# Small jobs off VectorE, double buffers for finished rows, two more closing steps and earlier gathers in a fused top-32 attention and top-1 expert kernel

## The chip, the cores and the metric

One core of one Trainium2 chip. Times are device microseconds (us) of one launch. TensorE (PE) does matmuls and transposes, VectorE (DVE), ScalarE (ACT) and GpSimd (POOL) do the rest, and SyncE (SP) issues most transfers. Indirect transfers (gathers and scatters by a list of rows) are issued by GpSimd.

## The reference

```python
scores = scale * np.matmul(q, k.transpose(0, 1, 3, 2))          # q, k, v: [8, 8, 576, 64], float32
kth = np.partition(scores, -32, axis=-1)[..., -32:-31]
scores = np.where(scores >= kth, scores, -1e9)
attn = softmax(scores)
x = np.matmul(attn, v).transpose(0, 2, 1, 3).reshape(4608, 512)
logits = x @ w_gate                                             # 8 experts
gate_w = softmax(logits) at the largest logit
out[token] = gate_w * (np.maximum(x @ w1[e], 0) @ w2[e])        # e: that expert; w1 [512, 1024], w2 [1024, 512]
```

So each row of scores keeps its 32 largest, and each token then goes through one of eight experts. All is float32; the kernel gets that precision from matmuls on split values (a high and a low part).

## The kernel before, in words

**Attention.** 144 steps, nine for each of 16 groups of head pairs; 18 steps make one batch. A step is spread over the loop by stages, so that iteration t works on several steps at once: TensorE computes the scores of step t+3 (L354, the rest in L367 and L373), ScalarE copies them to SBUF (L356, L375), VectorE finds the 32nd largest value of each row by MAX8 and match-replace rounds (L988 with 21 MAX8 a step, L994), GpSimd makes thresholds of it (L990), ScalarE takes the sign of score minus threshold (L429) and GpSimd adds it to the scores (L430), TensorE transposes (L443, L446), ScalarE takes the exponential (L451) and TensorE multiplies with the values (L460, L475).

**Small jobs.** Between these, small jobs run as generators in lanes: `prep` (inputs), `sums` (row sums of the exponentials), `rows` (finished rows of x are transposed, scaled and stored, with their gate logits), `find`, `redo` and `patch` (a batch's few rows whose mask by the approximate threshold was wrong are found, done again and scattered over the stored rows), `route` (each token's expert and slot in a table). Every `yield need(...)` names what the next piece costs on an engine, and `advance()` hands a piece out when the step has room (LIMITS L44, due times DUE L43). The pieces go through queues (`pe`, `vec`, `act`, `pool`) that are flushed into the engines at fixed places; all of them are recorded as L252. Instructions of an engine run in the order in which they were issued.

**Close and experts.** The loop runs on for closing iterations after the last scores; in those with t < steps + TADV one `advance(None)` hands out a piece of each lane without limits (L1009). Then the experts run by units: five early ones (units 0 to 4) with tokens of the first batches, so that they can start before the last batches are routed, then whole experts and leftovers. Unit 0 has its inputs (tiles kt) gathered and its weights split in the attention's close; other units gather theirs to gx (L841) by tables that `route` has scattered (L812). A unit has eight chunks: `hidden` (L1107), `project` (L1122), weight splits (L919, L921, L922), and in the later chunks the transposes of the next unit's inputs (L1087 to L1089). The remaining small jobs of the last batches run between these chunks. `fetch(u + 1)` is called from a unit's second chunk on, and `fetch(u + 2)` in its seventh chunk, though only for units that are not early (L1175).

The names that matter below: r_fl (in `find`, a list of slots), r_v and found (in `redo`, a count of values found again), hist and cum (in `route`, tokens per expert), vq and its sum with nr (in `sums`), xm, xl, lp and lpl (in `rows`), r_xa and r_hm (in `patch`).

## Time and profile before

| | us |
|---|---|
| three runs | 1322.58, 1326.03, 1327.28 (median 1326.03) |
| the profiled execution, its own time | 1327.61 |
| its span in the trace | 1325.8 |
| busy: TensorE / VectorE / ScalarE / GpSimd | 1265.1 / 1037.6 / 823.2 / 905.2 |
| mean granted TensorE clock | 0.985 |

Busy times are of the whole span, with attention up to about 785 us, a close and the experts' start up to about 820 us, and the experts from there. An engine that waits inside an instruction for something that the profile doesn't show counts as busy.

### The profile page before, as it was taken

What the parts mean: (1) busy time and instruction counts of PE and PEld (TensorE: products, weight loads), DVE (VectorE), ACT (ScalarE), POOL (GpSimd) and SP (SyncE); (2) the same over time, 40 slices, a digit from 0 to 9 for tenths busy, and PEclk for the clock granted to TensorE, in tenths of its full rate; (3) what the DMA queues carried; (4) which work ended last, traced back from release to release, by engine and by line L of the source; (5) the groups of instructions that cost most, each with busy time, mean ns of one, the idle gap of its engine ahead of it and who ended that gap; (6) DMA issues with size and microseconds to landing.
All of it is one profiled execution on the core that took longest, in us unless ns stands there. A gap on an engine that the chain in (4) does not pass through costs nothing.

```text
span 1325.8 us, 32793 instructions
## 1 busy us (share of the span) xinstructions
PE 1265.1 (95%) x9688; PEld 1007.6 (76%) x9688; DVE 1037.6 (78%) x6838; ACT 823.2 (62%) x1691; POOL 905.2 (68%) x1272
## 2 busy tenths in 40 slices
PE   5999999999999999999999988998999999999997
PEld 3677777777677777777676767888799898989996
DVE  6999999999999999999998985745673333345664
ACT  3998898888788788788887863433233323233442
POOL 3777886887887887888877886754654333245654
PEclk8999999999999999999999997999999999999999
DMA  6656564664655655555654434735654333246774
GB/s 169 202 161 175 172 206 142 174 187 147 174 173 162 169 166 161 170 167 162 173 164 134 150 119 113 221 91 159 157 178 154 109 109 115 88 151 189 219 218 124
DMA packets 271244, 211.25 MB, mean 159 GB/s; under 512 B 136216, under 2 KB 214216, under 8 KB 271056
## 3 DMA queue, kind: packets, MB, share of 16 engines
q1 hardware_dynamic: 260320, 185.92, 48.3%
q0 software_dynamic: 9504, 22.86, 5.4%
q8 instruction: 78, 1.28, 0.4%
q14 instruction: 110, 0.90, 0.2%
q10 hardware_dynamic: 1232, 0.30, 0.1%
HBM read 102.49 MB, written 107.90 MB: 159 GB/s over the span
## 4 chain that ended last, share of the span: by engine, by line
PE 62%; DVE 19%; issue 6%; POOL 5%; ACT 5%; DMA 2%; SPq 1%; POOLq 0%; ACTq 0%; DVEq 0%
PE ph L1107 16%; PE y L1122 15%; DVE cand L988 9%; PE ps L354 6%; PE px L460 6%; PE pt L252 5%; PE tt L446 5%; DVE cand L994 3%; DVE vq L994 3%; PE tt L443 3%; PE px L475 2%; ACT sg L429 2%; POOL sb L430 2%; PE mt L1087 1%; PE px L367 1%
## 5 line engine op out<-in xcount | busy, mean ns | idle before, releaser
L430 POOL TENSOR_TENSOR sb<-sb,sg 128x576 f32<-128x576 f32 x288 | 369.8, 1292 | 133.8 <-ACT sg L429 131.1
L988 DVE MAX8 cand<-sb 128x8 f32<-128x52 f32 (+2 forms) x3024 | 368.9, 211 | 2.8 <-ACT sb L356 2.2
L922 POOL TENSOR_TENSOR wl<-r,wh 128x512 fp32r<-128x512 f32 x110 | 142.4, 1296 | 221.2 <-DVE wh L921 211.8
L429 ACT ACTIVATE sg<-sb,nb 128x576 int8<-128x576 f32 x288 | 223.1, 775 | 23.6 <-POOL nb L990 21.5
L460 PEld LDWEIGHTS px<-et,rv 128*64 128x64 f32 x2688 | 132.1, 138 | 122.6 <-issue 57.5
L1108 ACT ACTIVATE hh<-ph 128x320 fp32r<-128x320 f32 (+3 forms) x136 | 58.3, 428 | 240.8 <-PE ph L1107 218.1
L994 DVE MAX8 vq<-cand 128x8 f32<-128x22 f32 (+7 forms) x1152 | 205.2, 207 | 0.8 <-DVE cand L994 0.8
L451 ACT ACTIVATE et<-tt 128x1152 f32<-128x1152 f32 x144 | 163.1, 1132 | 44.3 <-PE tt L446 43.5
L354 PE MATMUL ps<-qk 64*128 64x512 f32 (+1 forms) x576 | 183.9, 646 | 3.1 <-ACT sb L356 2.5
L1109 DVE SCALAR_TENSOR_TENSOR hl<-ph,hh 128x320 fp32r<-128x320 f32 (+3 forms) x136 | 65.1, 479 | 149.9 <-ACT hh L1108 128.9
L460 PE MATMUL px<-et,rv 128*64 128x128 f32 (+1 forms) x2688 | 166.7, 268 | 14.8 <-ACT xt L252 4.7
L356 ACT ACTIVATE sb<-ps 128x1024 f32<-128x1024 f32 x144 | 147.0, 1020 | 51.1 <-PE ps L354 48.1
L1107 PE MATMUL ph<-xh,wh 128*128 128x320 f32 (+3 forms) x536 | 168.3, 314 | 0.0
L446 PE MATMUL tt<-turner,sb 128*128 128x128 f32 x1296 | 166.5, 273 | 0.6 <-POOL sb L430 0.6
L1107 PE MATMUL ph<-xh,wl 128*128 128x320 f32 (+3 forms) x536 | 165.0, 308 | 0.0
L1107 PE MATMUL ph<-xl,wh 128*128 128x320 f32 (+3 forms) x536 | 164.7, 307 | 0.0
L994 DVE MATCH_REPLACE8 cand<-vq,cand 128x22 f32<-128x22 f32 (+2 forms) x864 | 157.8, 190 | 0.0
L446 PEld LDWEIGHTS tt<-turner,sb 128*128 128x128 f32 x1296 | 139.4, 141 | 1.0 <-POOL sb L430 1.0
L1122 PE MATMUL y<-wh,hh 128*128 128x512 f32 x324 | 128.2, 396 | 1.3 <-ACT yo L1126 1.3
L1122 PE MATMUL y<-wh,hl 128*128 128x512 f32 x324 | 128.4, 396 | 0.0
L1122 PE MATMUL y<-wl,hh 128*128 128x512 f32 x324 | 128.2, 396 | 0.0
L1107 PEld LDWEIGHTS ph<-xh,wh 128*128 128x128 f32 x536 | 101.2, 189 | 3.5 <-issue 0.6
(245 smaller groups left out, 2398.2 us busy)
## 6 DMA issues: line engine op xcount, KB each, us to landing
r<-in_moe_w_dram SPq DMA_DIRECT2D x220, 256.0 KB
sc<-sb SPq DMA_DIRECT2D x128, 288.0 KB
sc<-sb SPq DMA_DIRECT2D x128, 256.0 KB
rv<-in_v_dram SPq DMA_DIRECT2D x32, 256.0 KB
xs<-xm SPq DMA_DIRECT2D x16, 512.0 KB
rq<-in_q_dram SPq DMA_DIRECT2D x60, 128.0 KB
rk<-in_k_dram SPq DMA_DIRECT2D x60, 128.0 KB
sc<-sb SPq DMA_DIRECT2D x32, 144.0 KB
```

What stands on the lines that cost most here:

```text
L354: nc.tensor.matmul(MAINS[:, n], qk[:, 0, w], qk[:, 1, 2 * LEFT:], start=True, stop=True)
L356: nc.scalar.activation(bass.AP(EX[-1].tensor, EX[-1].offset, [list(EX[-1].ap[0]), [S + LEFT, 2], [1, M]]), MAINS, AF.Copy)
L429: nc.scalar.activation(upper(SG[i]), SB[u], AF.Sign, bias=nb[:, i, 1:2], accum_out=CNT[b][:, 2 * lt + i:2 * lt + i + 1])
L430: nc.gpsimd.tensor_tensor(SB[u], SB[u], SG[i], op=OP.add)
L446: nc.tensor.matmul(tt[:, c], x[:, c * 128:(c + 1) * 128], ident, start=False, stop=c in (3, 7, 8), is_transpose=True)
L451: nc.scalar.activation(ET[t], three.rearrange("p (c q) -> p c q", c=NB9), AF.Exp, scale=0.125)
L460: yield lambda kb=kb, blk=blk: nc.tensor.matmul(px[h * 64:(h + 1) * 64], block(rv, p % 2, kb if kb < MAIN else MAIN + n, h), et[:, blk, q] ...
L922: (nc.gpsimd if i else nc.vector).tensor_tensor(lo, r, hi, op=OP.subtract)
L988: one[m][0](*one[m][1])
L994: f(*a)
L1107: nc.tensor.matmul(ph, a[:, c, :], x[:, c, s], start=(m == 0), stop=(m == len(seq) - 1))
L1122: nc.tensor.matmul(PY[u, t], a[:, s], x, start=(f == 0 and m == 0), stop=(f == FC - 1 and m == 2))
```

## The change

- `TADV` goes from 5 to 7: two more closing iterations hand out a piece of each lane.
- In `rows`, the tiles xm, xl, lp and lpl get two buffers in place of one.
- In `find`, r_fl is made by ScalarE, right behind the copy that it reads, and one yield less.
- In `redo`, the count of found values goes from VectorE to three GpSimd instructions and one of ScalarE that accumulates; one yield of slack less, and the rest of VectorE's part has a cost of 1.2 in place of 1.6.
- In `route`, the copy of cum to hist goes from VectorE to GpSimd, two yields later.
- The last `sums` job starts in its step: its first two pieces are issued at once and the queues of GpSimd and ScalarE flushed.
- `fetch(u + 2)` is called in the seventh chunk of early units too.

```diff
-TADV = 5
+TADV = 7
...
-        xm = jobs.tile([128, 2 * MAIN, 128], F32, name="xm", bufs=1)
...
+        xm = jobs.tile([128, 2 * MAIN, 128], F32, name="xm", bufs=2)
...
         act(leave)
+        fl = sm("r_fl", [128, 1], I32)
+        act(nc.scalar.activation, fl, li[:, 1:2], AF.Identity, scale=float(NLT + 1), bias=li[:, 0:1])
         yield need(slack=1)
-        yield need(dve=0.1)
-        fl = sm("r_fl", [128, 1], I32)
-        vec(nc.vector.scalar_tensor_tensor, fl, li[:, 1:2], float(NLT + 1), li[:, 0:1], op0=OP.mult, op1=OP.add)
         yield need(pool=2.0)
...
-        v = sm("r_v", [128, 16])
+        v = sm("r_v", [128, 24])
         act(nc.scalar.activation, upper(SGR), sb, AF.Sign, bias=low, accum_out=nb[:, 4:5])
         yield need(slack=1)
-        yield need(slack=1)
-        yield need(dve=1.6)
+        yield need(pool=0.7)
+        pool(nc.gpsimd.tensor_scalar, v[:, 8:16], eight2, nb[:, 4:5], None, op0=OP.subtract)
+        pool(nc.gpsimd.tensor_tensor, v[:, 8:16], v[:, 8:16], v[:, 8:16], op=OP.mult)
+        pool(nc.gpsimd.tensor_scalar, v[:, 8:16], v[:, 8:16], 0.5, None, op0=OP.is_lt)
+        act(nc.scalar.activation, v[:, 16:24], v[:, 8:16], AF.Copy, accum_out=found[:, b:b + 1])
+        yield need(dve=1.2)
         vec(nc.vector.tensor_tensor, wk, SGR, sb, op=OP.subtract)
         vec(nc.vector.max, v[:, 0:8], wk)
-        vec(nc.vector.tensor_scalar, v[:, 8:16], eight2, nb[:, 4:5], None, op0=OP.subtract)
-        vec(nc.vector.tensor_tensor, v[:, 8:16], v[:, 8:16], v[:, 8:16], op=OP.mult)
-        vec(nc.vector.tensor_scalar, v[:, 8:16], v[:, 8:16], 0.5, None, op0=OP.is_lt, op1=OP.add,
-            accum_out=found[:, b:b + 1])
         vec(nc.vector.scalar_tensor_tensor, v[:, 8:16], v[:, 0:8], -BIG, v[:, 8:16], op0=OP.mult, op1=OP.mult,
             accum_out=nb[:, 3:4])
...
-        vec(nc.vector.tensor_copy, hist[:, :, KB], cum[:, :, KB])
         yield need(spot=1, pe=0.1, act=0.2)
...
         yield need(dve=0.7)
+        pool(nc.gpsimd.tensor_copy, hist[:, :, KB], cum[:, :, KB])
...
             start("sums", j_sums(m // NT), t + DUE['sums'])
+            if m == steps - 1 and len(lanes["sums"]) == 1:
+
+                for _ in range(2):
+                    wants["sums"] = next(lanes["sums"][0][1])
+                flush(gq)
+                flush(aq)
...
-            if f == FC - 2 and u >= first and u + 2 < len(units):
+            if f == FC - 2 and u + 2 < len(units):
                 fetch(u + 2)
```

The order of GpSimd's instructions in the close, behind the last pair of attention adds (L430), before:

```order
L430 TENSOR_TENSOR sb<-sb,sg_145 128x576
L252 IOTA pay 128x5
L840 MEMSET spacer 1x1
L841 DMA kt<-xs,ids_12840 128x512
...
L812 DMA table<-pay,pos 36864x4
L252 TENSOR_TENSOR vq<-vq,nr 128x576
L922 TENSOR_TENSOR rv_14005<-rq,rv_14004 128x512
L922 TENSOR_TENSOR kt<-rk,kt 128x512
L252 TENSOR_TENSOR vq<-vq 128x18x16
...
L252 TENSOR_SCALAR vq<-vq 128x18
L252 TENSOR_TENSOR r_xa<-r_xa,r_hm 128x512
L922 TENSOR_TENSOR wl_14136<-r_14093,wh_14135 128x512
```

The five scatters stand between the gathers of kt and the sum vq. The same place of GpSimd now:

```order
L430 TENSOR_TENSOR sb<-sb,sg_145 128x576
L252 TENSOR_TENSOR vq<-vq,nr 128x576
L252 TENSOR_TENSOR vq<-vq 128x18x16
L839 MEMSET spacer 1x1
L840 DMA kt<-xs,ids_12848 128x512
...
L252 TENSOR_SCALAR vq<-vq 128x18
L252 COPY hist<-cum 128x8
L252 IOTA pay 128x5
L921 TENSOR_TENSOR rv_14015<-rq,rv_14014 128x512
L921 TENSOR_TENSOR kt<-rk,kt 128x512
L810 MEMSET spacer 1x1
L811 DMA table<-pay,pos 36864x4
...
L252 TENSOR_TENSOR r_xa<-r_xa,r_hm 128x512
L252 DMA r_at<-atab,r_fl 128x4
```

There are two gathers of kt and five scatters to table in both. The sum vq now stands ahead of the gathers and the scatters; the weight splits rv and kt (L922 before, L921 now), which stood behind the scatters, stand ahead of them, and the product r_xa right behind them.

The order of TensorE's instructions there, from the last matmul of `find` (r_qx) to the first expert matmul, before:

```order
L252 MATMUL pt_235<-rhs,r_qx 128x2
L252 LDWEIGHTS ones
L252 MATMUL pt_236<-hist,ones 128x8
L1087 MATMUL mt<-turner,kt 128x128 x4
L1087 MATMUL ph<-turner,kt 128x128 x4
L1107 MATMUL ph<-xh,rv_14004 128x256
```

The transposes of unit 0's inputs (kt) follow at once. TensorE now:

```order
L252 MATMUL pt_235<-rhs,r_qx 128x2
L252 MATMUL pt_236<-turner,r_xa 128x128 x4
L252 MATMUL pt_235<-wg,r_et 128x8 x4
L252 LDWEIGHTS ones
L252 MATMUL pt_236<-hist,ones 128x8
L252 MATMUL pt_235<-turner,xt 128x144 x3
L1092 MATMUL mt<-turner,kt 128x128 x4
L1092 MATMUL ph<-turner,kt 128x128 x4
L1112 MATMUL ph<-xh,rv_14014 128x256
```

The transposes of r_xa, the gate logits of the patched rows and the first turns of the last rows stood behind unit 0's first chunk; they now stand ahead of the transposes of unit 0's inputs (kt).

## Rows read from the trace of the kernel before

**Rows 1.** Busy time of each engine in stretches of the span (the answer by windows; columns: stretch, its length, then the busy us and instructions of PE, PEld (weight loads), DVE, ACT and POOL, the granted TensorE clock, the DMA share and GB/s).

```profile
581.00:679.00 98.00, 95.32 (x869) 70.31 (x866) 97.89 (x795) 81.85 (x171) 81.93 (x119) 1.00 0.58 167
...
780.00:800.00 20.00, 16.33 (x172) 12.70 (x168) 9.21 (x40) 8.24 (x20) 16.09 (x26) 1.00 0.23 63
800.00:860.00 60.00, 53.09 (x323) 47.14 (x323) 40.92 (x83) 23.99 (x50) 43.25 (x59) 0.89 0.62 178
...
1000.00:1168.00 168.00, 168.00 (x956) 151.74 (x955) 58.81 (x107) 49.05 (x97) 60.36 (x64) 1.00 0.37 114
```

**Rows 2.** Groups of VectorE's instructions over the whole span (columns: line, engine, operation, out<-in, shapes, count, busy us, mean ns of one, idle before).

```profile
L252 DVE SCALAR_TENSOR_TENSOR r_fl<-r_li 128x1 int32<-128x1 f32 x8 | 11.3, 1407 | 0.0
...
L252 DVE COPY hist<-cum 128x8 bf16<-128x8 bf16 x8 | 5.9, 740 | 0.1
...
L252 DVE TENSOR_SCALAR r_v<-eight,r_nb 128x8 f32<-128x8 f32 x8 | 5.7, 710 | 0.0
```

**Rows 3.** The same view for one batch period of the attention loop, 483.4 to 581.4 us.

```profile
L252 DVE SCALAR_TENSOR_TENSOR r_fl<-r_li 128x1 int32<-128x1 f32 x1 | 2.4, 2354 | 0.0
...
L252 DVE COPY hist<-cum 128x8 bf16<-128x8 bf16 x1 | 1.1, 1076 | 0.0
...
L252 DVE TENSOR_SCALAR r_v<-eight,r_nb 128x8 f32<-128x8 f32 x1 | 0.3, 315 | 0.0
```

**Rows 4.** The timeline of all engines around one r_fl (columns: start us, duration us, engine, line, operation, out<-in, shapes, count).

```profile
528.78 2.53 POOL L430 TENSOR_TENSOR sb<-sb,sg 128x576 f32<-128x576 f32 x2
...
528.98 2.35 DVE L252 SCALAR_TENSOR_TENSOR r_fl<-r_li 128x1 int32<-128x1 f32 x1
```

**Rows 5.** All waits of TensorE from 581 to 679 us (columns: who, line, released by whom: us in total, times, longest).

```profile
PE px L460 <- issue: 1.0, 2, 0.5
PE px L460 <- ACT xt L252: 0.9, 1, 0.9
PE pt L252 <- ACT r_et L252: 0.4, 1, 0.4
PE pt L252 <- ACT po L252: 0.3, 1, 0.3
```

**Rows 6.** All waits of VectorE from 300 to 700 us, same columns.

```profile
DVE cand L988 <- issue: 0.3, 2, 0.2
```

**Rows 7.** TensorE's timeline in the close; in brackets the idle time before a row and what ended it.

```profile
785.14 0.23 PE L252 MATMUL pt<-hist,before 128*128 128x40 bf16 x1 [2.04 <-DVE hist L252]
...
803.54 1.97 PE L460 MATMUL px<-et,rv 128*64 128x128 f32 x16 [4.18 <-ACT et L451]
...
807.50 0.38 PE L252 MATMUL pt<-rhs,r_qx 128*128 128x2 bf16 x8 [1.26 <-DVE r_qx L252]
...
807.76 1.09 PE L1087 MATMUL mt<-turner,kt 128*128 128x128 f32 x4
...
810.40 0.58 PE L1107 MATMUL ph<-xh,rv 128*128 128x256 f32 x1 [0.69 <-ACT xh L1088]
```

**Rows 8.** GpSimd's timeline in the close.

```profile
787.94 2.52 POOL L430 TENSOR_TENSOR sb<-sb,sg 128x576 f32<-128x576 f32 x2 [2.40 <-ACT sg L429]
...
790.78 1.05 POOL L841 DMA_INDIRECT kt<-xs,ids  x1 [0.16 <-issue]
...
793.39 1.00 POOL L812 DMA_INDIRECT table<-pay,pos  x1 [0.22 <-issue]
...
798.54 0.90 POOL L812 DMA_INDIRECT table<-pay,pos  x1 [0.22 <-issue]
799.46 1.20 POOL L252 TENSOR_TENSOR vq<-vq,nr 128x576 f32<-128x576 f32 x1
803.09 1.65 POOL L922 TENSOR_TENSOR rv<-rq,rv 128x512 fp32r<-128x512 f32 x1 [2.43 <-DVE rv L921]
805.10 1.26 POOL L922 TENSOR_TENSOR kt<-rk,kt 128x512 fp32r<-128x512 f32 x1 [0.36 <-DVE kt L921]
...
810.18 1.04 POOL L252 TENSOR_TENSOR r_xa<-r_xa,r_hm 128x512 f32<-128x512 f32 x1
...
818.23 1.29 POOL L922 TENSOR_TENSOR wl<-r,wh 128x512 fp32r<-128x512 f32 x1 [0.96 <-DVE wh L921]
...
819.71 1.07 POOL L841 DMA_INDIRECT gx<-xs,ids  x1 [0.16 <-issue]
```

**Rows 9.** ScalarE's timeline there.

```profile
800.69 0.68 ACT L252 ACTIVATE vq<-vq 128x576 f32<-128x576 f32 x1 [8.68 <-issue]
...
801.33 0.62 ACT L919 ACTIVATE rv<-rq 128x512 fp32r<-128x512 f32 x1
```

**Rows 10.** TensorE's timeline where the inputs of units 3 and 4 are first transposed.

```profile
902.70 0.63 PE L1087 MATMUL mt<-turner,gx 128*128 128x128 f32 x4 [3.40 <-DMA gx<-xs,ids]
...
941.09 0.63 PE L1087 MATMUL mt<-turner,gx 128*128 128x128 f32 x4 [1.71 <-DMA gx<-xs,ids]
```

**Rows 11.** GpSimd's timeline, the first gather of each of these two units.

```profile
897.10 0.98 POOL L841 DMA_INDIRECT gx<-xs,ids  x1 [0.18 <-issue]
...
935.64 1.24 POOL L841 DMA_INDIRECT gx<-xs,ids  x1 [0.17 <-issue]
```

**Rows 12.** Groups of GpSimd's instructions over the whole span (columns as in rows 2).

```profile
L922 POOL TENSOR_TENSOR wl<-r,wh 128x512 fp32r<-128x512 f32 x110 | 142.4, 1296 | 221.2 <-DVE wh L921 211.8 <-issue 7.6 <-DMA r<-in_moe_w_dram 1.2
...
L990 POOL TENSOR_TENSOR nb<-vq,factors 128x4 f32<-128x4 f32 x144 | 28.4, 197 | 4.8 <-DVE vq L994 4.8
```

**Rows 13.** TensorE's timeline in unit 0, where the moved work stood, and the first transposes of unit 1's inputs.

```profile
817.23 0.90 PE L252 MATMUL pt<-turner,xt 128*128 128x144 f32 x6
817.96 0.60 PE L252 MATMUL pt<-turner,r_xa 128*128 128x128 f32 x4
...
824.81 0.60 PE L1087 MATMUL mt<-turner,gx 128*128 128x128 f32 x4
```

**Rows 14.** Two stretches at the lower granted clock (columns as in rows 1).

```profile
801.72:815.37 13.65, 9.73 (x56) 8.42 (x57) 8.49 (x13) 5.00 (x10) 7.29 (x9) 0.50 0.46 118
904.12:907.53 3.41, 3.41 (x12) 3.12 (x11) 1.14 (x3) 1.01 (x2) 0.90 (x1) 0.50 0.89 232
```

More of the change, by code (lines that the diff above doesn't have):

```diff
@@ L515, in j_rows @@
         b = 2 * n // HP
-        xm = jobs.tile([128, 2 * MAIN, 128], F32, name="xm", bufs=1)
-        xl = jobs.tile([128, 128], F32, name="xl", bufs=1)
-        lp = jobs.tile([128, 2 * MAIN, 2 * E], F32, name="lp", bufs=1)
-        ll_ = jobs.tile([128, 2 * E], F32, name="lpl", bufs=1)
+        xm = jobs.tile([128, 2 * MAIN, 128], F32, name="xm", bufs=2)
+        xl = jobs.tile([128, 128], F32, name="xl", bufs=2)
+        lp = jobs.tile([128, 2 * MAIN, 2 * E], F32, name="lp", bufs=2)
+        ll_ = jobs.tile([128, 2 * E], F32, name="lpl", bufs=2)
         pts = {}
```

## The prediction

> **What bounds the kernel now.** I read the stretches first, because the span has three regimes [rows 1]. In the attention loop (200 to 757 us, of which 581:679 is one batch period of 98 us) VectorE is busy 97.89 us and TensorE 95.32 us of 98: two engines look full. From 780 to 800 us neither is (TensorE 16.33 of 20, VectorE 9.21); that is the close, where the last attention steps hand over to the experts. From 1000 us TensorE is busy 168.00 us of 168, and nothing that the change touches can help there except an earlier start.
>
> The question in the loop is which of the two full engines sets the pace. The busy time of VectorE there holds waiting: a 128x1 operation, r_fl, has a mean of 1407 ns over the run and takes 2354 ns in one period, where r_v, eight times as wide, takes 315 [rows 2, 3]. Beside r_fl, GpSimd runs a pair of L430 adds from 528.78 to 531.31; r_fl starts at 528.98 and ends at 531.33, with the pair [rows 4]. So these operations are slow because GpSimd is at work, and they end when it ends. The table of waits then shows what TensorE waits for in a period: 2.6 us, for ScalarE (xt, r_et, po) and for issue, and nothing for VectorE [rows 5]. In 400 us VectorE itself waits 0.3 us [rows 6]. VectorE is full, but nobody is seen waiting for it. I take TensorE with ScalarE and GpSimd behind it as the loop's pace, and VectorE as an engine that stretches to fit.
>
> At the close the idle rows of TensorE say what ends last [rows 7]: 2.04 us for hist, 4.18 us for et, 1.26 us for r_qx, then 0.69 us until the first expert matmul at 810.40. The 4.18 us are a queue: ScalarE stands still for 8.68 us before the exponential vq at 800.69 [rows 9], which needs GpSimd's vq add at 799.46, which stands behind two kt gathers and five table scatters (issued from 790.78 on; the last ends at 799.44) [rows 8]. After that come two plain waits: 3.40 and 1.71 us for gathers of expert inputs, issued 5.6 and 5.5 us before [rows 10, 11].
>
> **VectorE's small jobs, taken away.** r_fl (8 x 1407 ns = 11.3 us), the hist copy (8 x 740 = 5.9 us) and the found-count of redo (its largest piece 8 x 710 = 5.7 us) leave VectorE [rows 2]: 22.9 us over the run, and in one period 2.354 + 1.076 + 0.315 = 3.7 us [rows 3]. They go to ScalarE and GpSimd, as instructions on 1 to 8 columns. If TensorE sets the pace, what can come back is at most its idle time, 2.6 us a period over the some five periods from 200 to 700 us: 13 us, if every one of these waits went. None is for VectorE, so the likely value is near 0. The other end: ScalarE and GpSimd get about 0.2 us an instruction (GpSimd's 128x4 nb takes 0.2 us on average [rows 12]), four of GpSimd's and two of ScalarE's a batch, so up to 1.2 us a batch. ScalarE's share, 0.4 us, could lengthen the TensorE waits on xt and r_et: 5 x 0.4 = +2 us. I take -1 us, nearest to the waits of rows 5. The found-count adds a wait: VectorE's last r_v operation now needs GpSimd's three. Queued behind it is a top-k step, whose sums ScalarE's sign reads much later; with 0.6 us of GpSimd work ahead of it I cost it at nothing, and the cover is VectorE's lack of waiters. The Trainium skill (SBUF — State Buffer, Who interferes with whom) says that VectorE and GpSimd share a port pair as an exclusive lock, the second one blocked until the first is done. By that rule r_fl's 2.35 us are held time, and the trace agrees; the next two-input VectorE operation can inherit it, which again makes the saving smaller than 3.7 us a period.
>
> The double buffers of xm, xl, lp and lpl remove no wait that these rows show; I cost them at nothing.
>
> **The close, reordered.** GpSimd now does the last sums job at once: vq add ahead of the kt gathers and of the scatters. The add then starts when the last L430 pair ends, at 790.4, instead of 799.46. The exponential follows at about 791.7 (add 1.20 us), the et copies no longer queue behind it, and the 4.18 us shrink to about 1.5 (et waits its own transposes). That is -2.7 us, and the 2.04 us for hist goes too, though GpSimd's L430 chain, not TensorE, paces the steps there, so I count it at 0 (bound -2).
>
> But two more closing steps put the next patch ahead of unit 0. TensorE must now transpose r_xa, do the gate logits and three xt turns before its kt turns. r_xa is a GpSimd product that stands behind the five scatters and, before these, the weight splits rv and kt. Those splits ended at 806.36 because ScalarE was late; now ScalarE casts rv at about 797 and the splits end near 802.8 (two operations, 2.9 us). Five scatters (6.4 us by those from 793.39 to 799.44, one per 1.29) end at 809.2, r_xa (1.04) at 810.2. Transpose, copy, logits and xt take 0.6 + 0.6 + 0.4 + 0.5 = 2.1 us, and turns to first expert matmul 810.40 - 807.76 = 2.64 us: 815.0, which is +4.6 against 810.40 [rows 7, 8]. About 2.1 us of that work was done later before (r_xa at 817.96, xt at 817.23, [rows 13]) and is saved there. Net +2.5 us. With splits 3 us earlier it is -0.5; with them as late as before it is +6.
>
> Unit 1's gather is issued behind a weight split, 9.3 us after the first expert matmul (819.71) and lands for the turn at 824.81, 5.1 us later, with no wait [rows 8, 13]. If the first matmul moves by 4.6 and the turn by only 2.5, the turn waits 2.1 us at most; I take 0.5.
>
> The clock was 0.50, the 1.2 GHz level, from 801.72 to 815.37, after the 4.18 us of idle [rows 14]. With another gap of some 5 us in the same place I expect a like stretch, and count nothing (bounds -4 for none of it, +2 for a longer one). Close: +3 us, from -3 to +7.
>
> **The gathers.** With the condition on unit number gone, the inputs of units 2, 3 and 4 are fetched three of a unit's eight chunks sooner, into the buffer that the unit before last has left. Two such gathers stand 38.5 us apart (897.10 and 935.64 [rows 11]), so three chunks are about 14 us, against waits of 3.40 and 1.71. Both waits go: -5.1 us. After the first, TensorE ran at 0.50 from 904.12 to 907.53, 3.41 us with twelve matmuls that would take half [rows 14]: -1.7 us. A third gather moves the same way, and its wait was 0. GpSimd issues as many gathers as before; what moves behind them is weight splits, with 221.2 us of idle ahead of theirs [rows 12]. Sum -6.8 us; if the low clock comes back elsewhere, -5.1.
>
> **Sum.** -1 + 3 - 6.8 = -4.8 us. The profiled execution took 1327.61 us, so 1322.8 by its own time; the median of the runs before is 1326.03, 1.58 below that execution, and from there the same sum gives 1321.2, which I predict. A measurement tells 0.3%, 4.0 us, from no change; the sum lies just beyond it.
>
> **Rivals.**
> 1. VectorE sets the loop's pace. Then 3.7 us a period come back over five periods and some at both ends: -20 us, with the rest about 1302. For: 97.89 of 98 us busy, more than TensorE. Against: rows 5 and 6, and the held time. The Trainium skill (Perfetto Trace Analysis, Identifying the Most-Contended Engine) calls the engine with the highest occupancy the one to improve, and counts matmul busy time for little; by that rule VectorE's saving is the gain. The waits speak against it here. Chance 0.07.
> 2. The close costs more than the gathers give: r_xa behind the scatters. Its price is the wait of the transposes on GpSimd's product plus a longer stretch at half clock: +7, +2 and a gather wait of 2.1 make +11 - 6.8 = +4, about 1330. It decides if r_xa ends after 814 us. For: in the new order every scatter stands ahead of the product. Against: ScalarE reaches rv earlier. Chance 0.15.
> 3. The close gains: the 4.18 us go altogether and with them the half clock (-4.2 - 4), and some of TensorE's waits in the loop. With the gathers -12 to -16 us, about 1312. For: it is what the order of vq says. Against: r_xa. Chance 0.2.
> 4. The gathers' wait only moves: TensorE then waits for ScalarE or for weights, which come at a fixed pace; the sum is within 2 us of 0, 1325. Chance 0.1. Against it: after 1000 us TensorE has no idle at all [rows 1].
>
> **How the numbers follow.** Forecast 0.48, rivals 0.07, 0.15, 0.2, 0.1. The forecast's own spread, about 3 us, crosses the 0.3% bound: 0.28 of its 0.48 is faster, 0.2 is the same. Rivals 1 and 3 are faster (0.27), rival 4 the same (0.1), rival 2 slower in 0.11 and the same in 0.04. Faster 0.55, same 0.34, slower 0.11. The range runs from rival 3 to rival 2, 1310 to 1330, and leaves out rival 1 and the tails.
>
> **What would show it.** No 128x1 r_fl on VectorE; its busy share in the loop stays above 96% or its idle rows now name the scores, while a batch period stays within 1 us of 98: right. A period of 94 to 95 us: rival 1. At the close: et no longer waits behind vq, but a wait of TensorE on r_xa of 4 to 6 us stands just ahead of the kt turns. No gx wait before units 3 and 4, and no stretch at 0.50 near 905. If TensorE shows no wait on r_xa, the close was mis-sized; if gx waits remain, the fetch was not sooner.

## The result, and the profile after

The changed kernel took 1336.91 us, median of four runs (1333.68, 1336.12, 1337.71, 1337.77), against 1326.65 of the four before beside it (1322.58, 1326.03, 1327.28, 1327.71). The ratio is 1.0076, 95% interval 1.0054 to 1.0097: slower, where the forecast was faster, and outside its range. The profiled execution took 1333.68 us (span 1331.5). Cut at two marks that both traces have, the end of the last L430 pair and the first expert matmul:

| span of the profiled execution, us | before | after | moved by | forecast |
|---|---|---|---|---|
| start to the end of the last L430 pair | 790.46 | 793.84 | +3.4 | -1 |
| from there to the first expert matmul | 19.94 | 29.46 | +9.5 | +4.6 |
| from there to the end | 515.42 | 508.22 | -7.2 | -8.4 |

The forecast column is the prediction's own sum, with the 2.1 us that it gave back and the 0.5 us of unit 1's gather put where they fall. The sum is +5.7 in place of -4.8. Both misses lie ahead of the first expert matmul.

By windows (columns as in [rows 1]; the first row is one batch period of the attention, from step 108's scores to step 126's):

```profile
570.61:669.37 98.76, 94.91 (x864) 69.99 (x863) 93.21 (x790) 82.16 (x174) 82.73 (x123) 1.00 0.58 166
...
800.00:860.00 60.00, 42.63 (x284) 36.57 (x283) 33.81 (x72) 20.29 (x45) 40.19 (x65) 0.89 0.47 141
...
1000.00:1168.00 168.00, 168.00 (x958) 151.71 (x957) 59.34 (x108) 49.64 (x98) 57.09 (x62) 1.00 0.38 113
```

VectorE is busy 93.21 us of the period in place of 97.89 [rows 1], so the jobs did leave it: r_fl takes ScalarE 295 ns and the copy to hist GpSimd 219 ns on average, against 1407 and 740 on VectorE [rows 2]. The period is not shorter for it: 98.76 us, where before has 97.90 between the same two steps. From 800 to 860 us TensorE has 42.63 us of work where it had 53.09.

What VectorE waits for from 300 to 700 us (columns as in [rows 6], which held nothing but 0.3 us):

```profile
DVE r_v L252 <- ACT r_v L252: 22.1, 4, 5.7
DVE cand L987 <- DVE vq L993: 0.3, 1, 0.3
```

This is the found-count, once a batch, and besides it 0.3 us. Its timeline, all engines, 560 to 572 us:

```profile
562.66 0.74 DVE L252 TENSOR_TENSOR r_wk<-sg,r_sb 128x576 f32<-128x576 bf16 x1
...
563.44 0.76 DVE L252 MAX8 r_v<-r_wk 128x8 f32<-128x576 f32 x1
...
567.79 0.32 POOL L252 TENSOR_SCALAR r_v<-eight,r_nb 128x8 f32<-128x8 f32 x1
...
569.61 0.22 ACT L252 ACTIVATE r_v<-r_v 128x8 f32<-128x8 f32 x1
569.96 0.17 DVE L252 SCALAR_TENSOR_TENSOR r_v<-r_v 128x8 f32<-128x8 f32 x1 [5.61 <-ACT r_v L252]
```

VectorE is ready for the operation that needs the count at 564.35 (569.96 less the 5.61 us in brackets). GpSimd, which takes its queue in order, comes to the first of its three small instructions at 567.79, ScalarE follows, and VectorE goes on at 569.96. The 0.6 us of instructions cost VectorE 5.61 us, and the top-k step is behind them in its queue.

The close, TensorE's timeline (answers to [rows 7]):

```profile
808.11 0.35 PE L252 MATMUL pt<-rhs,r_qx 128*128 128x2 bf16 x8 [2.65 <-DVE r_qx L252]
815.16 1.11 PE L252 MATMUL pt<-turner,r_xa 128*128 128x128 f32 x4 [6.70 <-POOL r_xa L252]
816.96 1.87 PE L252 MATMUL pt<-wg,r_et 128*128 128x8 f32 x8 [0.69 <-ACT r_et L252]
818.69 0.17 PE L252 MATMUL pt<-hist,ones 128*128 128x8 bf16 x1
819.10 1.81 PE L252 MATMUL pt<-turner,xt 128*128 128x144 f32 x6 [0.24 <-ACT r_lr L252]
820.70 1.06 PE L1092 MATMUL mt<-turner,kt 128*128 128x128 f32 x4
821.56 1.06 PE L1092 MATMUL ph<-turner,kt 128*128 128x128 f32 x4
823.30 0.38 PE L1112 MATMUL ph<-xh,rv 128*128 128x256 f32 x1 [0.69 <-ACT xh L1093]
...
838.11 0.66 PE L1092 MATMUL mt<-turner,gx 128*128 128x128 f32 x4 [2.03 <-DMA gx<-xs,ids]
```

The 4.18 us for et [rows 7] have become 1.39, and 6.70 us for r_xa stand in their place. Then r_xa's chain takes 5.54 us (815.16 to 820.70) before the kt turns start. The 2.03 us at 838.11 are unit 1's inputs; the waits of [rows 10] for units 3 and 4 are gone. The first expert matmul takes 0.38 us, where the same took 0.58 us in before [rows 7]: it now runs at the full clock. GpSimd there (answers to [rows 8]):

```profile
793.80 1.18 POOL L252 TENSOR_TENSOR vq<-vq,nr 128x576 f32<-128x576 f32 x1
...
803.50 1.64 POOL L921 TENSOR_TENSOR rv<-rq,rv 128x512 fp32r<-128x512 f32 x1 [2.12 <-DVE rv L920]
805.51 1.26 POOL L921 TENSOR_TENSOR kt<-rk,kt 128x512 fp32r<-128x512 f32 x1 [0.36 <-DVE kt L920]
...
806.96 2.05 POOL L811 DMA_INDIRECT table<-pay,pos  x1 [0.17 <-POOL spacer L810]
...
813.13 0.91 POOL L811 DMA_INDIRECT table<-pay,pos  x1 [0.23 <-issue]
814.05 1.05 POOL L252 TENSOR_TENSOR r_xa<-r_xa,r_hm 128x512 f32<-128x512 f32 x1
...
832.68 1.27 POOL L840 DMA_INDIRECT gx<-xs,ids  x1 [0.16 <-issue]
```

The sum vq did start with the end of the last pair, as forecast. r_xa ends at 815.10, past the 814 us at which rival 2 was said to decide. ScalarE's rows say why the splits were not at 800:

```profile
801.15 0.69 ACT L252 ACTIVATE r_xa<-pt,r_nb 128x512 f32<-128x512 f32 x1 [2.27 <-PE pt L252]
801.74 0.62 ACT L918 ACTIVATE rv<-rq 128x512 fp32r<-128x512 f32 x1
```

The cast of rv, which I had put at 797, stands behind the patch's own r_xa, which waits for TensorE.

### The profile page after: what moved, and what is told of

It is laid out like the page before. It is cut to its first block, busy times and chain, and to the rows that moved or that the text cites. A ratio compares the mean times of both kernels' runs of the same rounds, so it can differ in the third digit from the quotient of the medians.

```text
span 1331.5 us, 32778 instructions
## 1 busy us (share of the span) xinstructions
PE 1259.2 (95%) x9688; PEld 1002.1 (75%) x9688; DVE 1008.0 (76%) x6790; ACT 826.7 (62%) x1715; POOL 908.9 (68%) x1304
## 4 chain that ended last, share of the span: by engine, by line
PE 68%; ACT 9%; POOL 8%; issue 5%; DVE 5%; SPq 2%; DMA 2%; another core or an unknown queue 0%; POOLq 0%; ACTq 0%; DVEq 0%
PE ph L1112 17%; PE y L1127 16%; PE ps L354 7%; PE pt L252 7%; PE px L460 6%; PE tt L446 6%; ACT sg L429 3%; POOL sb L430 3%; PE tt L443 3%; ACT sb L356 2%; DVE cand L987 2%; PE px L475 2%; ACT qk L252 1%; PE px L367 1%; PE mt L1092 1%
## 5 line engine op out<-in xcount | busy, mean ns | idle before, releaser
L430 POOL TENSOR_TENSOR sb<-sb,sg 128x576 f32<-128x576 f32 x288 | 372.8, 1304 | 130.5 <-ACT sg L429 106.2
L921 POOL TENSOR_TENSOR wl<-r,wh 128x512 fp32r<-128x512 f32 x110 | 142.6, 1297 | 225.1 <-DVE wh L920 218.8
L460 PE MATMUL px<-et,rv 128*64 128x128 f32 (+1 forms) x2688 | 163.1, 267 | 9.4 <-ACT xt L252 7.2
```

The source lines that it names most:

```text
L430: nc.gpsimd.tensor_tensor(SB[u], SB[u], SG[i], op=OP.add)
L460: yield lambda kb=kb, blk=blk: nc.tensor.matmul(px[h * 64:(h + 1) * 64], block(rv, p % 2, kb if kb < MAIN else MAIN + n, h), et[:, blk, q] ...
L921: (nc.gpsimd if i else nc.vector).tensor_tensor(lo, r, hi, op=OP.subtract)
```

## The experiments

All 16 runs in one table: the batch period, then the same three parts of the span, of each profiled run, and the ratio to the kernel before on the same chip. These chips ran the kernel before at 1320.5 to 1321.75 us. No trace of it is at hand from them; the kernels whose attention code is that of before (fetch, close, sums + fetch) have a period of 96.4 us there, against 97.90 in the trace of before from the first chip.

| run | period | to last pair | to first expert matmul | to the end | ratio (95%) |
|---|---|---|---|---|---|
| e1 change, redo of before | 97.5 | 788.50 | 29.24 | 508.3 | 1.0043 (1.0030 to 1.0057) |
| e2 change, r_xa ahead of the scatters | 98.7 | 797.40 | 24.46 | 515.3 | 1.0097 (1.0082 to 1.0113) |
| e3 before + fetch | 96.41 | 783.90 | 19.92 | 510.2 | 0.9965 (0.9951 to 0.9978) |
| e4 = e2 with redo of before | 97.5 | 788.18 | 23.43 | 512.6 | 1.0026 (1.0012 to 1.0039) |
| e5 before + r_fl, hist moved, steps kept | 96.43 | 783.82 | 20.08 | 519.4 | 1.0023 (1.0014 to 1.0033) |
| e6 before + r_fl moved, one step less | 97.54 | 788.73 | 24.73 | 526.6 | 1.0147 (1.0127 to 1.0166) |
| e7 before + new redo | 98.67 | 787.54 | 19.93 | 510.1 | 0.9995 (0.9984 to 1.0006) |
| e8 before + close (TADV, sums) | 96.43 | 783.19 | 24.79 | 511.6 | 1.0013 (1.0002 to 1.0025) |
| e9 before + new redo, one step later | 98.5 to 101.8 | 796.2 | 16.5 | 510.0 | 1.0059 (1.0038 to 1.0081) |
| e10 change, find's step kept, old redo | 96.39 | 783.50 | 25.09 | 506.0 | 0.9976 (0.9967 to 0.9985) |
| e11 before + early sums + fetch | 96.43 | 783.56 | 20.54 | 509.3 | 0.9959 (0.9946 to 0.9971) |
| e12 = e4, unit 1's gather first | 97.5 | 787.88 | 24.39 | 510.3 | 1.0033 (1.0020 to 1.0046) |
| e13 before + redo's added instructions | 96.79 | 782.96 | 19.92 | 510.0 | 0.9968 (0.9956 to 0.9980) |
| e14 the change again | 98.61 | 796.99 | 29.46 | 510.5 | 1.0134 (1.0120 to 1.0149) |
| e15 = e10 with TADV 5 | 96.43 | 785.01 | 20.54 | 511.9 | 0.9964 (0.9952 to 0.9977) |
| e16 = e10 with single buffers | 96.40 | 784.74 | 25.07 | 506.2 | 0.9967 (0.9954 to 0.9980) |

### The loop: the found-count (e1, e7, e13, e9)

**e1**: the change, with redo's code as it was before.

```diff
-        yield need(pool=0.7)
-        pool(... v[:, 8:16] ...)    # three on GpSimd, one on ScalarE
-        yield need(dve=1.2)
+        yield need(slack=1)
+        yield need(dve=1.6)
+        vec(... v[:, 8:16] ..., accum_out=found[:, b:b + 1])
```

> The changed kernel with the count of redo back on VectorE and its two steps of slack, as before. Theory A (VectorE's last redo operation now waits 5.6 us a period for ScalarE's r_v, and the late top-k then holds GpSimd and ScalarE): that wait is gone, a batch period falls from 98.7 to 97.9-98.0 us, the last L430 pair ends near 790.5 instead of 793.8, and the time falls by about 3 us. Theory B (the loop is longer because ScalarE and GpSimd got more small work, or for another reason): the period falls by 0.2 us at most and the time by under 1 us.

The period came down from 98.7 to 97.5 us and the last pair from 793.84 to 788.50 us; beside e2 and e14, which have the new redo, it is 8.9 and 8.5 us earlier. The kernel is still slower than before.

**e7**: the reverse, the kernel before with the new redo alone (the same lines as in the change).

> The kernel before with the change's redo alone (count on GpSimd and ScalarE, one yield of slack less). Theory A (VectorE waits there for ScalarE's r_v): a wait of 1.5 to 5 us a period on r_v and a period 0.5 to 1.2 us longer, 3 to 8 us slower than the kernel before. Theory B (the wait comes only with find one step earlier): wait under 0.5 us, time within 2 us.

The same wait appears with nothing else changed; VectorE's waits and the windows of one period:

```profile
DVE r_v L252 <- ACT r_v L252: 4.4, 1, 4.4
```

```profile
566.53:665.20 98.67, 96.20 (x864) 70.96 (x863) 94.28 (x791) 82.06 (x173) 82.93 (x122) 0.98 0.57 165
```

The period is 98.67 us, but its clock is 0.98; in the one period of this run without a stretch at the lower level it is 97.08. The total is even with before (0.9995) although the last pair ends 3.6 us later than in e3: the part behind the first expert matmul, 510.1 us, is as short as e3's without e3's edit; more on that under the gathers.

**e13**: before, with the three GpSimd instructions and the one of ScalarE added on a scratch tile, and VectorE counting as before. It takes the wait away and leaves the added work.

```diff
+        pool(nc.gpsimd.tensor_scalar, w[:, 0:8], eight2, nb[:, 4:5], None, op0=OP.subtract)
+        pool(... w ...)    # two more
+        act(nc.scalar.activation, w[:, 8:16], w[:, 0:8], AF.Copy, accum_out=w[:, 16:17])
         yield need(dve=1.6)
         vec(...)           # as before
```

> The kernel before with the change's three GpSimd instructions and one of ScalarE added to redo on a scratch tile, at the places of the change (one slack yield replaced), while VectorE counts as before: the same added work and the same order of matmuls as in redo alone, and no new wait of VectorE. Theory A (VectorE's wait of 4.4 us lengthens the period): period 96.4 to 96.8 us, last L430 pair within 1 us of 784. Theory B (the added instructions on GpSimd and ScalarE do): 97 us or more, as in redo alone.

VectorE's waits in one period, and its windows:

```profile
DVE xm L252 <- ACT sb L356: 0.7, 1, 0.7
DVE r_key L252 <- ACT sg L429: 0.6, 1, 0.6
```

```profile
563.84:660.63 96.79, 94.63 (x865) 70.03 (x864) 95.23 (x792) 82.02 (x173) 81.98 (x122) 1.00 0.58 169
```

The wait for r_v is gone and the period is 0.4 us above 96.4. So the added instructions cost at most 0.4 us a period. VectorE's part of redo stands at the same place of its queue as in e7, so what e7 has beyond this goes with the wait: 0.3 us in the period at the full clock (97.08), 1.9 us in the one shown, which has a stretch at the lower clock. That the wait brings this stretch is not shown. In the changed kernel, with a wait of 5.6 us and the clock at 1.00, the new redo costs 1.2 us a period (98.7 against e1's 97.5).

**e9**: before with the new redo and one more step of slack ahead of VectorE's part.

```diff
+        yield need(slack=1)
         yield need(dve=1.2)
```

> The kernel before with the change's redo, and VectorE's part of it one step later (a yield of slack before it), so that ScalarE and GpSimd have the same new instructions as in the run of redo alone and only the wait goes. Theory A (VectorE's wait for r_v makes the period 98.6 there): no wait on r_v over 0.5 us, period 96.4-96.9 us. Theory B (the new small instructions on GpSimd and ScalarE make it): period still 98 us or more.

The wait for r_v fell to 0.8 us, but VectorE now waited 1.7 us for GpSimd's vq in the same period (up to 2.9 us in others), and the periods were 98.5 to 101.8 us: the extra step moved other jobs too, the scatters to table by two steps. Theory A's number missed; the run decides nothing about the cause.

### The loop: find's dropped step (e6, e5, e10)

**e6**: before, with r_fl on ScalarE as in the change and the one yield less.

```diff
+        fl = sm("r_fl", [128, 1], I32)
+        act(nc.scalar.activation, fl, li[:, 1:2], AF.Identity, scale=float(NLT + 1), bias=li[:, 0:1])
         yield need(slack=1)
-        yield need(dve=0.1)
-        fl = sm("r_fl", [128, 1], I32)
-        vec(nc.vector.scalar_tensor_tensor, fl, ...)
```

> The kernel before with r_fl on ScalarE as in the change, its yield dropped: find's gathers r_at, r_nb and r_sb come one step sooner, beside two table scatters, and redo one step sooner too. Theory A (this move alone loads two GpSimd steps in a row, so that sign waits 2.9 us for nb and TensorE 1.5 us for qk): a period is 0.8 to 1.1 us longer than that of the fetch alone (96.4), 4 to 6 us slower than the kernel before. Theory B (the hist copy, the double buffers or r_fl on ScalarE cause it): within 2 us of the kernel before.

It is the slowest kernel of all, 1.0147. GpSimd's timeline in one period shows what a yield less does:

```profile
626.70 1.03 POOL L811 DMA_INDIRECT table<-pay,pos  x1 [0.16 <-issue]
628.04 1.00 POOL L252 DMA_INDIRECT r_at<-atab,r_fl  x1 [0.30 <-issue]
629.34 0.96 POOL L252 DMA_INDIRECT r_nb<-ntab,r_fl  x1 [0.31 <-issue]
...
630.84 2.55 POOL L430 TENSOR_TENSOR sb<-sb,sg 128x576 f32<-128x576 f32 x2
...
633.73 1.00 POOL L811 DMA_INDIRECT table<-pay,pos  x1 [0.20 <-issue]
...
635.21 1.01 POOL L252 DMA_INDIRECT r_sb<-sc,r_at  x1 [0.17 <-issue]
...
640.18 0.20 POOL L989 TENSOR_TENSOR nb<-vq,factors 128x4 f32<-128x4 f32 x1
```

Find's gathers, handed out one step sooner, now fall into steps that have a scatter to table already, two such steps in a row; in before r_at and r_nb share their step with a scatter and r_sb does not. The thresholds nb come late, ScalarE's sign waits (6.1 us for nb in this period, 3.5 in one of e3), and TensorE after it:

```profile
640.42 0.78 ACT L429 ACTIVATE sg<-sb,nb 128x576 int8<-128x576 f32 x1 [2.90 <-POOL nb L989]
```

```profile
643.65 0.66 PE L252 MATMUL pt<-turner,rk 128*128 128x128 f32 x4 [1.51 <-ACT qk L252]
```

That is 1.1 us a period (97.54 against 96.4), 5 us up to the last pair, and 5 us more in the close. About half of its loss lies behind the first expert matmul (526.6 us), where TensorE waits 8.2 us for VectorE's xl and 2.7 us for its hl.

**e5**: the same two jobs off VectorE (r_fl and the copy to hist), with a step of slack in place of the dropped one, so that the steps stay where they were.

```diff
+        act(nc.scalar.activation, fl, ...)
         yield need(slack=1)
+        yield need(slack=1)
-        vec(nc.vector.scalar_tensor_tensor, fl, ...)
...
+        pool(nc.gpsimd.tensor_copy, hist[:, :, KB], cum[:, :, KB])
```

> The kernel before with r_fl on ScalarE and the copy of hist on GpSimd, and one yield of slack put in so that find's later pieces (the gathers r_at and r_nb) stay in their steps: in the loop VectorE loses 3.4 us a period and nothing else moves. Theory A (VectorE does not set the loop's pace): the period stays within 0.4 us of the run of the fetch alone (96.4 us), the time within 3 us of the kernel before. Theory B (VectorE sets it): 2 to 3.4 us less a period, 10 us or more faster. Theory C (the small instructions on ScalarE and GpSimd cost more than they save): 0.5 to 1 us more a period, 3 to 5 us slower.

Two periods, that of e3 (VectorE's work as before) and that of e5:

```profile
563.58:659.99 96.41, 94.62 (x865) 70.01 (x864) 94.30 (x791) 81.75 (x171) 81.07 (x119) 1.00 0.58 169
```

```profile
563.18:659.61 96.43, 94.62 (x864) 70.01 (x864) 93.50 (x795) 82.00 (x172) 81.34 (x120) 1.00 0.59 169
```

The two jobs on VectorE in that period of e3 (columns as in [rows 2]):

```profile
L252 DVE COPY hist<-cum 128x8 bf16<-128x8 bf16 x1 | 0.6, 630 | 0.0
...
L252 DVE SCALAR_TENSOR_TENSOR r_fl<-r_li 128x1 int32<-128x1 f32 x1 | 0.1, 141 | 0.0
```

So e5 took 0.8 us a period off VectorE and not 3.4: its busy time falls by just that, and the period does not move by 0.1 us. In the loop of before on the first chip the same two took 2.35 + 1.08 us [rows 3], since r_fl was held there beside GpSimd's adds; from 300 to 700 us of e3, e8, e11 and e13, where it has the same place in VectorE's order, it took 0.14 us. For e3's loop rival 1 is out. For the first chip's loop, with VectorE full and r_fl held, no run tests it. The Trainium skill (Perfetto Trace Analysis, Identifying the Most-Contended Engine) would have the engine with the highest occupancy improved first, and does not judge TensorE by its matmul busy time; by that it is VectorE here (94.30 of 96.41 us), and e5 measures nothing for 0.8 us less of it. As a whole e5 is 3 us slower than before: its first two parts are those of e3, and behind them TensorE waits 7.2 us for gathers of expert inputs.

**e10**: the change with the step kept and redo as before.

> The changed kernel with both loop moves taken back: find's pieces keep their steps (a yield of slack behind r_fl) and redo counts on VectorE as before; r_fl and hist stay off VectorE, the double buffers, TADV 7, the early sums and the earlier fetch stay. Theory A (the two moves are the whole loss in the loop): period 96.4 us, last L430 pair near 784, and with the fetch's 5 us against a close 5 us longer the time is within 3 us of the kernel before, some 10 us below the changed kernel. Theory B (something else of the change also lengthens the loop): period over 97 us.

Period 96.39 us and 0.9976: with these two edits undone the change is faster than before. The loop's loss is those two.

### The close (e2, e4, e12, e8, e15, e16)

**e2** and **e4**: r_xa's product flushed into GpSimd ahead of the last batch's scatters, in the change and in e1.

```diff
             if c == 0 or b not in ahead:
                 yield need(pool=1.0)
+            if c == 0 and b in ahead and b == max(ahead):
+                flush(gq)
```

> The changed kernel with one GpSimd row moved: the product r_xa of the last patch is issued ahead of the last five table scatters, not behind them. Theory A (TensorE's 6.70 us wait before r_xa's transposes is the queue of scatters): the wait falls below 1 us, the first expert matmul comes at 816-817 instead of 823.3, the time falls by 6 to 8 us. Theory B (ScalarE's casts and the splits set the close, so that another wait takes its place, by the table or by unit 1's gather): the first matmul moves by less than 3 us or a gather wait grows by as much, the time falls by under 2 us.

> The changed kernel with both edits: redo's count back on VectorE and r_xa ahead of the scatters. Theory A (two added waits explain the loss, and add up): 9 to 11 us faster than the changed kernel, so level with or faster than the kernel before by 0 to 2 us. Theory B (they overlap, or neither is the cause): under 5 us faster than the changed kernel.

TensorE in e4:

```profile
803.49 1.09 PE L252 MATMUL pt<-turner,r_xa 128*128 128x128 f32 x4
...
811.61 0.58 PE L1114 MATMUL ph<-xh,rv 128*128 128x256 f32 x1 [0.69 <-ACT xh L1095]
...
831.14 1.12 PE L1094 MATMUL mt<-turner,gx 128*128 128x128 f32 x4 [2.93 <-DMA gx<-xs,ids]
```

The 6.7 us wait is gone and the first expert matmul stands 5.8 us nearer to the last pair than in e1 (23.43 against 29.24); in e2 5.0 us against the change. So the scatters ahead of r_xa cost 5 to 6 us of the close. But 4.3 us of them are lost again after the first matmul in e4 (512.6 against 508.3), and e4 is still slower than before (1.0026), where theory A had it level or faster. The 2.93 us wait for unit 1's inputs is not what took them: e1 waits 2.86 us there. The clock is. The 32.25 us behind the first expert matmul, in e1 and in e4 (columns as in [rows 1]):

```profile
817.75:850.00 32.25, 27.51 (x178) 24.27 (x179) 22.88 (x54) 11.76 (x26) 17.34 (x25) 0.95 0.57 175
```

```profile
811.61:843.86 32.25, 27.46 (x154) 24.05 (x155) 19.90 (x46) 10.23 (x21) 18.88 (x31) 0.82 0.63 190
```

The granted clock is 0.95 in e1 and 0.82 in e4, and 0.13 of 32.25 us is 4.2 us. In e1 the stretch at the lower level was over by the first expert matmul (0.38 us), and half of it had gone by while TensorE waited for r_xa; in e4 it still held there (0.58 us for the same matmul).

**e12**: e4 with unit 1's gather called right behind unit 0's.

```diff
         fetch(0)
+        fetch(1)
         load_w(2)
```

> The run with r_xa ahead of the scatters and redo's old count, and in addition unit 1's gather issued ahead of unit 0's first weight splits. Theory A (what r_xa first won was given back because unit 1's gather stands behind the same GpSimd queue): its wait of 2.9 us is gone, from the first expert matmul to the end takes 509 to 510 us in place of 512.6, 2 to 4 us faster than that run. Theory B (weights or the low clock take it): under 1 us.

The wait for unit 1's inputs is gone and the part behind the first matmul 2.3 us shorter, but that matmul came 1.0 us later, and the total is as in e4. The gather is therefore not what kept e4 from its gain.

**e8**: before with the two closing steps and the early sums, and nothing else of the change.

> The kernel before with the close alone: TADV 7 and the early start of the last sums; the five scatters stand here ahead of the splits, r_xa behind both. Theory A (more closing steps put the patch ahead of unit 0 and cost more than the early sum gives): first expert matmul 3 to 7 us later against the last L430 pair than the 20 us of the kernel before, a TensorE wait on r_xa of 2 to 6 us, 2 to 6 us slower. Theory B (the close gains, the loss is all in the loop): 2 us or more faster.

The close is 4.9 us longer than e3's (24.79 against 19.92), with 0.49 us of wait for r_xa, and the total only 1.0013; without a trace of before from that chip it is not shown where the rest comes back. The moved chain costs 5 us of close by itself; the wait of 6.7 us comes only together with find's dropped step (e6, where TADV is 5, has one of 7.4).

**e15** and **e16**: e10 with TADV back at 5, and e10 with one buffer for xm, xl, lp and lpl.

> The run with both loop moves taken back, and TADV at 5 again. Theory A (the two more closing steps lose: 25.1 us from the last L430 pair to the first expert matmul against 20.5 with TADV 5): 1 to 3 us faster than that run. Theory B (the work moved ahead is saved later, 506.0 us to the end against 509.3): within 1 us, or slower.

> The run with both loop moves taken back, and xm, xl, lp and lpl with one buffer as before. Theory A (the double buffers change nothing): within 1 us of that run, period 96.4 us. Theory B (they let finished rows be stored without a wait): 2 us or more slower, with a wait of VectorE on xm or lp.

The ratios of e10, e15 and e16 are 0.9976, 0.9964 and 0.9967, with intervals that overlap: none can be told from another. TADV 5 shortens the close by 4.6 us and the part behind it is 5.9 us longer, which comes to nothing, closest to theory B of e15. The double buffers do nothing that can be seen.

### The gathers, and the best version (e3, e11)

**e3**: before with the one condition of fetch changed.

```diff
-            if f == FC - 2 and u >= first and u + 2 < len(units):
+            if f == FC - 2 and u + 2 < len(units):
```

> The kernel before with the earlier fetch of early units alone. Theory A: the gx waits of 3.40 and 1.71 us and the stretch at half clock near 905 are gone, nothing else moves, 6.8 us faster than the kernel before (5.1 without the clock). Theory B (TensorE then waits for weights or ScalarE instead): within 2 us of the kernel before.

All waits of TensorE for gx are gone and the kernel is faster, by 4.6 us against an interval of 2.9 to 6.5 us. The size depends on the rest, though: without the new condition these waits are 5.1 us in before, 7.2 in e5, 2.7 in e7 and 2.0 in e13, and e13 alone, which changes no gather, comes out 4.2 us faster than before, with 510.0 us behind the first expert matmul. The condition removes the wait, whatever its size; how much of e3's gain would come without it is not shown.

**e11**: before with the early sums and the new condition.

> The kernel before with the earlier fetch and the early start of the last sums, TADV left at 5, so that the patch stays behind unit 0. Theory A (the early sums alone take the 2.5 us wait for et and the queue behind vq out of the close): first expert matmul 17 to 19 us behind the last L430 pair in place of 19.9, 1 to 3 us faster than the fetch alone. Theory B (the splits and the scatters behind them set the close): within 1 us of the fetch alone.

1314.98 us, 0.9959 (0.9946 to 0.9971), the fastest version of all; e3, on another chip, is at 0.9965, so the early sums add nothing that can be told apart, as theory B had it.

### The whole again (e14)

> The changed kernel itself, timed again beside the kernel before. By the parts measured so far on these chips: loop +10 to +14 us (find's step +4.8, redo +5 to +9), close +10 less 2 given back, gathers -5.2: 12 to 16 us slower than the kernel before. If the loop's loss were that of the first pair of profiles (3.4 us), 6 us slower.

TensorE's wait in the close of this run:

```profile
818.30 1.12 PE L252 MATMUL pt<-turner,r_xa 128*128 128x128 f32 x4 [6.68 <-POOL r_xa L252]
```

17.7 us slower than before on that chip. With e3's first two parts for those of before, whose code they share, and 515.42 us from the trace of before for the third, the parts are +13.1 to the last pair, +9.5 in the close, -4.9 behind: +17.7. On the first chip the close is the same +9.5 and the loop only +3.4, since before had a period of 97.90 there.

## Why the prediction was wrong

- **What bounds the loop.** VectorE's busy time does hold waiting: the same instructions took 97.89 us of a period on the first chip [rows 1] and 94.30 in e3. That work taken off it gives nothing back is shown for 0.8 us (e5). That its other operations would inherit r_fl's held time did not come: from before to after VectorE's busy time fell by more than 4 us a period, for 3.7 us of jobs [rows 3]. Wrong was the step after it: "I cost it at nothing, and the cover is VectorE's lack of waiters". That nobody was seen waiting for VectorE says at most that a shorter VectorE gains nothing, not that a longer one costs nothing. I counted 0.6 us of GpSimd instructions; what stands in the row is the time until GpSimd and then ScalarE come to them, 5.6 us. Over the loop that is 5.3 us from e1 to the changed kernel's first trace, 8.5 to e14 and 8.9 to e2 (788.50 against 793.84, 796.99 and 797.40), against 0.
- **find's dropped yield** has no price in the prediction at all. The term for r_fl counted the instruction and not the gathers r_at, r_nb and r_sb behind it, which moved one step sooner on GpSimd's queue. Measured: 1.1 us a period, 5 us up to the last pair (e6, e1), and in the close the order in which the scatters fall behind the weight splits, 4.8 us in e6.
- **The close: direction right, size wrong.** Forecast: first expert matmul 24.5 us behind the last pair (815.0 - 790.46); measured 29.46. Of the 4.9 us, 1.5 are r_xa's end (21.3 us behind the pair in place of 19.7): 0.6 for the splits, as ScalarE's cast of rv stood behind the wait of r_xa for TensorE, and 0.9 for the scatters, the first of which took 2.05 us. The other 3.4 are the chain from r_xa's transposes to the kt turns, 5.54 us where I summed 2.1. I took full-clock durations, 0.60 us for the four transposes [rows 13], in a stretch that I forecast at the lower level, where they took 1.11. Two terms were too small even at the full level: the three xt turns are all six matmuls of the row of 0.90 us [rows 13], not half of them, and the gate logits take 0.96 us in before, where I had 0.4 without a row. From row to row, transposes and copy take 1.80 us against 1.2, the gate logits 2.14 against 0.4, the xt turns 1.60 against 0.5. From 806 to 815 us the granted clock was 0.66 and from 815 to 824 us 0.58. The kt turns, costed from rows at that level, took 2.60 us against 2.64.
- **The gathers: right**, on the size with some luck. No wait for units 3 and 4, no lower clock near 905, and e3 is 4.6 us faster against 6.8. What is left is 2.0 us for unit 1, at the 2.1 us bound. The -7.2 us of the third part hold more than gathers: in before the lower clock reached 5.0 us past the first expert matmul (810.40 to 815.37 [rows 7, 14]), in after it did not, and half of that, 2.5 us, is the clock's by this estimate.
- **The double buffers** are worth nothing, as forecast (e16). **The early vq** took the 4.18 us for et down to 1.39, as forecast, but its -2.7 us were not earned: in e11 TensorE waits 2.7 us for r_qx and 2.0 for r_et in et's place, and the time stays that of e3.
- **The rivals.** Rival 2 happened, by its own sign (r_xa after 814 us), and was priced as if the loop stayed as it was; its 1330 is 7 us below the measured median. No rival let the loop become slower, and both slow edits stand in the diff as changed yields: find lost one, and in redo a yield for GpSimd's piece took the place of one, so that VectorE's part kept its step and found the count not yet made.

**Open:** why the same attention code runs with a period of 97.90 us on the first chip and 96.4 in e3, e8 and e11 elsewhere. The traces differ in r_fl's held time (2.35 against 0.14 us) and in VectorE, full there and with 2.1 us to spare in e3; whether the held time makes the longer period or comes of it, no run tells, and if it makes it, taking r_fl off VectorE did gain something on that chip. Open too is why the part behind the first expert matmul is 510 us in e7, e9 and e13, without the new condition, and 519 and 527 in e5 and e6. The waits are seen, 2.7, 3.8 and 2.0 us for gx in the first three, 7.2 for gx in e5 and 8.2 for xl in e6; what makes them differ is not.

## What to carry to other kernels

An engine that is full in the profile with nobody waiting for it need not gain from losing work, and can still lose by a wait: price a moved job by when the other engines' queues come to it, not by its instructions. An instruction's time in one trace may be held time; look at a second trace before it is put into a sum. A yield or a line of slack is a place in every engine's order: when one goes, list all that moves with it, the indirect transfers first. And a chain that moves into a stretch at the lower clock is costed with rows of that level; a wait taken out of such a stretch can come back as slower matmuls behind it.

## What the runs showed of the hardware

- An operation of VectorE can be held beside GpSimd's adds in one execution and run free in another: r_fl took 2.35 us in the first chip's loop, where it began just behind the start of a pair of adds and ended with it [rows 4], and 0.14 us in the same batches of e3, e8, e11 and e13. On ScalarE it takes 0.295 us on average. The Trainium skill (SBUF — State Buffer, Who interferes with whom) has one of two such operations block fully while the other holds the shared ports; that r_fl ends with the adds agrees, though no run here shows the port itself.
- A round trip over two engines (VectorE to GpSimd to ScalarE and back) for three 128x8 operations was 5.6 us when these engines were busy with work of their own.
- Five scatters issued one behind the other came some 1.3 us apart, as in [rows 8], but the first of them held GpSimd for 2.05 us, beside 0.91 for the last.
- The granted clock fell within the loop in e7 (0.98 over a period) and was 1.00 in every other period whose windows are quoted here. At the lower level the four r_xa transposes took 1.11 us and six xt matmuls 1.81, at the full level 0.60 and 0.90 [rows 13].
